# Soft-capped attention with soft mixture of experts: pairs alternating by tile, one PV pass per pair, and a five-step exponential on VectorE

## The chip, the cores and the metric

The kernel runs on one core of one Trainium2 chip. The metric is device time in microseconds, the median of several runs. The profile and the trace are of one execution; their times count from its first instruction, and the span in them (313.8 us) is about 2 us shorter than the measured time. In the text PE is the matrix engine (PEld its weight loads), ACT the engine for activations, DVE the vector engine, POOL the general-purpose one, and SP issues transfers.

## What is computed

```python
# q, k, v: (8, 12, 448, 64) float32, cap = 30
scores = q @ k.T / sqrt(64)
scores = cap * tanh(scores / cap)
attn = softmax(scores)                       # over keys
x = (attn @ v) -> (3584, 768)                # heads side by side
logits = x @ phi                             # (3584, 32): 8 experts, 4 slots each
d = softmax over tokens(logits);  slot_input = d.T @ x
h = relu(slot_input[e] @ w1[e]);  slot_out = h @ w2[e]
c = softmax over slots(logits);   out = c @ slot_out          # (3584, 768) float32
```

Almost all of the work by element is in the 8 x 12 x 448 x 448 scores, each of which needs one tanh and one exponential. As the scores are capped at 30, no maximum is subtracted.

## The kernel before

Heads are taken in pairs: 48 of them, and two pairs (four heads) make a quad `Q`, whose two pairs `h = 0, 1` lie on partitions 0-63 and 64-127 of `kT` and `qT`. A pair has NT = 7 tiles; a tile is 64 keys of each of its two heads against 448 queries. Tiles are numbered in a row, pair by pair. A chunk is CS = 3 tiles (one tanh instruction), a batch `j` is CH = 6 tiles (one exponential). There are 336 tiles, 112 chunks, NCH = 56 batches; one of the eight sequences takes PER = 7 batches.

```python
def qk_chunk(i):                               # scores of three tiles
    sc = psS.tile([P, CS, 512], F32, ...)      # two such buffers, a bank per tile
    for u in range(CS):
        pr, c = divmod(i * CS + u, NT)         # pair and tile
        Q, h = divmod(pr, 2)
        r = slice(h * HP, h * HP + HP)         # row half of the array
        for n in range(2):                     # the pair's two heads: column halves
            cs = slice(n * HP, n * HP + HP)
            pe.matmul(sc[cs, u, 0:S], qkT["k", Q][r, c, cs], qkT["q", Q][r, :, cs], ...)

def tanh_chunk(i):
    exs[j] = exps[j % 4].tile([P, CH, S], BF16)          # four buffers
    act.activation(exs[j][...], sc[...], ACT.Tanh, scale=qk_scale / cap)

def exp_chunk(j):                              # one tile fewer where DVE takes it
    exp_part(j, 1 if j in shared else 0, CH)

shared = [j for j in range(NCH - 2) if j % 7 in (1, 3) and j > 7]

def poly_exp(j, part):                         # on DVE, tile 0 of batch j, in float32
    # 7 operations: scale to a power of two in int32, mask the mantissa, mask the exponent,
    # then four multiply-adds in float32
```

"PV" is the product of the exponentials with `v`. A column of ones beside each head's `v` gives the sum for the softmax, so a head has 65 columns and a pair VW = 130. The queries are taken in NG = 4 groups of 128, of which the last begins at 320 and repeats 64 queries of the third (masked out later). A pair takes two passes of two groups, each into the one `pv` bank and each followed by its norm:

```python
GOFF = (0, 128, 256, 320)
def pv_tiles(pr, half, c0, c1, home=None):
    for c in range(c0, c1):
        for n in range(2):
            g = 2 * half + n
            pe.matmul(pvs[pr, half][:, n, 0:VW], exs[j][:, u, GOFF[g]:GOFF[g] + P],
                      vbds[Q % 2][:, h, c, :], ...)

def norm(pr, half):
    dve.reciprocal(rec, pv[:, :, :, DH:DH + 1])                          # 128 x 4
    dve.tensor_tensor(xq[Q][...], pv[:, :, :, 0:DH], rec..., op=ALU.mult)  # 128 x 256
```

The loop over the batches, in which `run(j, slot)` calls the rest of the work put into the slots (transposes of k, q and x, `logits`, `slot_sums`, loads, the parts of `poly_exp`, and `spare(n)`: n matmuls of 128 columns on ones whose result nothing uses):

```python
for j in range(NCH):
    run(j, "0")                               # e_exp, the exponential of a sequence's logits
    tanh_chunk(2 * j)
    tanh_chunk(2 * j + 1)
    exp_chunk(j - 1)                          # the first ones differ
    pv_pass(pr, 0)                            # pr: the pair whose last tile lies in batch j - 2
    run(j, "a")
    qk_chunk(2 * j + 2)
    run(j, "b")
    pv_pass(pr, 1)
    run(j, "c")
    qk_chunk(2 * j + 3)
    run(j, "d")
# then the last two pairs, the last logits and slot sums, the two layers of the experts, the output
```

Of the kernel before, what the change touches and what calls it, by code (L numbers as in the profile page):

```python
# [11 lines left out]
I32 = mybir.dt.int32  # L12
ALU = mybir.AluOpType
# [3 lines left out]
P = 128  # L17
HP = 64
# [6 lines left out]
GOFF = (0, 128, 256, 320)  # L25
VW = 2 * (DH + 1)
MASKED = -30000.0

POW2 = (0.013534163, -0.157022653, 12.3105704, 23.0539684, 37.6797712)
# [3 lines left out]
def kernel(  # L33
# [45 lines left out]
    mask = consts.tile([P, NG, NS], F32, name="mask")  # L79
    pool.memset(mask, 0.0)  # L80
    pool.memset(mask[0:HP, NG - 1, :], MASKED)
# [40 lines left out]
    for n0 in range(R2, len(blocks), 4):  # L122
        t = dram.tile([P, 2, 4, HD], BF16, name=f"w2d{n0}")
        for half in range(2):
# [3 lines left out]
    hpad = consts.tile([P, E, NFT, NS], BF16, name="hpad")  # L128

# [4 lines left out]
    px = att.enter_context(tc.tile_pool(name="px", bufs=1))  # L134

    xe, xm, xp = (px.tile([P, S], dt, name=nm)
                  for nm, dt in (("xe", I32), ("xm", F32), ("xp", F32)))
    qk = att.enter_context(tc.tile_pool(name="qk", bufs=2))
    exps, vb = [], []
    for nm, home in (("ex0", exps), ("ex1", exps), ("vb0", vb), ("ex2", exps), ("ex3", exps),  # L140
                     ("vb1", vb)):
        home.append(att.enter_context(tc.tile_pool(name=nm, bufs=1)))
# [4 lines left out]


# [124 lines left out]
    def qk_chunk(i):  # L273
        sc = psS.tile([P, CS, 512], F32, name="sc", tag="sc")
        scores[i] = sc
        for u in range(CS):
            pr, c = divmod(i * CS + u, NT)
            Q, h = divmod(pr, 2)
            r = slice(h * HP, h * HP + HP)
            for n in range(2):  # L280
                cs = slice(n * HP, n * HP + HP)
                pe.matmul(sc[cs, u, 0:S], qkT["k", Q][r, c, cs],  # L282
                          qkT["q", Q][r, :, cs], start=True, stop=True)

    def tanh_chunk(i):
        j, half = divmod(i, CH // CS)
        if half == 0:
            exs[j] = exps[j % 4].tile([P, CH, S], BF16, name="ex", tag="ex")
# [13 lines left out]
    shared = [j for j in range(NCH - 2) if j % 7 in (1, 3) and j > 7] if cap < 80 else []  # L302

    def poly_exp(j, part):
        t, bits = exs[j][:, 0, :], 2.0 ** 23
        if part == 0:
            dve.tensor_scalar(xe, t, cap * math.log2(math.e) * bits,
                              (127 + math.log2(POW2[0])) * bits, ALU.mult, ALU.add)
            dve.tensor_scalar(xm.bitcast(I32), xe, 0x007FFFFF, 0x3F800000,
                              ALU.bitwise_and, ALU.bitwise_or)  # L310
            dve.tensor_scalar(xe, xe, -0x00800000, None, ALU.bitwise_and)
        elif part == 1:
            dve.scalar_tensor_tensor(xp, xm, POW2[1], xm, ALU.add, ALU.mult)
            dve.scalar_tensor_tensor(xp, xp, POW2[2], xm, ALU.add, ALU.mult)
        else:
            dve.scalar_tensor_tensor(xp, xp, POW2[3], xm, ALU.add, ALU.mult)
            dve.scalar_tensor_tensor(t, xp, POW2[4], xe.bitcast(F32), ALU.add, ALU.mult)

    def pv_tiles(pr, half, c0, c1, home=None):

        Q, h = divmod(pr, 2)
        if c0 == 0:
            if h == 0 and half == 0:
                xq[Q] = xs.tile([P, NG, 2 * P], BF16, name="xq", tag="xq")
            pvs[pr, half] = psV.tile([P, 2, VW], F32, name="pv", tag="pv") \
                if home is None else home
        for c in range(c0, c1):
            j, u = divmod(pr * NT + c, CH)
            for n in range(2):
                g = 2 * half + n  # L330
                pe.matmul(pvs[pr, half][:, n, 0:VW],  # L331
                          exs[j][:, u, GOFF[g]:GOFF[g] + P],
                          vbds[Q % 2][:, h, c, :],
                          start=(c == 0 and n == 0), stop=(c == NT - 1),
                          skip_group_check=True)

    def norm(pr, half):
        Q, h = divmod(pr, 2)
        pv = pvs.pop((pr, half))[:, :, 0:VW].rearrange("p g (i w) -> p g i w", i=2)
        rec = xs.tile([P, 2, 2, 1], F32, name="rec", tag="rec", bufs=4)  # L340
        dve.reciprocal(rec, pv[:, :, :, DH:DH + 1])  # L341
        dve.tensor_tensor(  # L342
            xq[Q][:, 2 * half:2 * half + 2, h * P:(h + 1) * P]
            .rearrange("p g (i d) -> p g i d", i=2),
            pv[:, :, :, 0:DH],
            rec.to_broadcast([P, 2, 2, DH]), op=ALU.mult)

    def pv_pass(pr, half, home=None):
        pv_tiles(pr, half, 0, NT, home)
        norm(pr, half)  # L350


    def x_transp(pr):
        Q, h = divmod(pr, 2)
        ps = psT.tile([P, NG, P], BF16, name="xps", tag="T")
        for g in range(NG):
            pe.transpose(ps[:, g, :], xq[Q][:, g, h * P:(h + 1) * P], ident)  # L357
        t = xs.tile([P, NG, P], BF16, name="xT", tag="xT", bufs=2)
        dve.tensor_copy(t, ps)  # L359
        xTs[pr] = t  # L360

    def logits(Q, ps=None):
# [3 lines left out]
        for g in range(NG):  # L366
            for h in range(2):
                pe.matmul(ps[:, g, :], xTs[2 * Q + h][:, g, :],
                          phib[:, 2 * hq + h, :], start=(h == 0), stop=(h == 1))
# [3 lines left out]
        dve.tensor_tensor(lgs[b], ps, mask if hq == 0 else lgs[b], op=ALU.add)  # L373
# [14 lines left out]
    def e_norm(b):  # L388

        ps = psT.tile([P, 1], F32, name="zps", tag="T")  # L390
        for g in range(NG):
            pe.matmul(ps, e4s[b][:, g, :], ones[:, 0:1], start=(g == 0), stop=(g == NG - 1))
# [7 lines left out]
    def e_transp(b):  # L400

        ps = psT.tile([P, 512], BF16, name="eps", tag="T")
        for g in (3, 0, 1, 2):
            pe.transpose(ps[:, GOFF[g]:GOFF[g] + P], e4s[b][:, g, :], ident)
# [12 lines left out]
    def slot_mms(b, ps, gs, jts=None):  # L417
        for g in gs:
            for jt in range(NJ):
                pe.matmul(ps[:, jt, :],  # L420
                          xq[b * NQB + jt // 2][:, g, (jt % 2) * P:(jt % 2 + 1) * P],
                          es[b][:, g, :], start=(g == 0 and jt == 0), stop=(g == NG - 1),
                          skip_group_check=True)
# [15 lines left out]
    aux = {}  # L439
# [5 lines left out]

    def spare(n):

        busy(n, psV.tile([P, 2, VW], F32, name="junk", tag="pv")[:, 0, 0:P])

    PER = 2 * NQB * NT // CH  # L450
# [10 lines left out]
    for b in range(B):  # L461
# [3 lines left out]
        else:  # L465
            quad_in(3 * b + 1, (j - 1, "b"), (j, "a"), (j - 1, "d"), (j, "c"), (j + 1, "d"))
        quad_in(3 * b + 2, (j, "d"), (j + 1, "c"), (j + 2, "b"), (j + 2, "d"),
                (j + 4, "d"))
        quad_in(3 * b + 3, (j + 4, "a"), (j + 5, "a"), (j + 3, "d"), (j + 5, "c"),
                (j + 6, "d"))  # L470
        p = 6 * b
        at(j + 1, "d", spare, 34 if b == 0 else 10)
        at(j + 2, "d" if b == 0 else "a", spare, 4 if b == 0 else 14)
        if b:
            at(j + 2, "c", spare, 8)
        at(j + 3, "d", spare, 10 if b == 0 else 4)
        at(j + 4, "a", x_transp, p)
        at(j + 5, "a", x_transp, p + 1)
        at(j + 6, "a", x_transp, p + 2)
        at(j + 5, "d", logits, 3 * b)  # L480
        if b < B - 1:
            at(j + 7, "a", x_transp, p + 3)
            at(j + 8, "a", x_transp, p + 4)
            at(j + 7, "d", logits, 3 * b + 1)
# [334 lines left out]
```

The softmax here doesn't subtract the row's maximum and nothing guards it: scores larger than these inputs give would overflow.

## Time and profile before

| | |
|---|---|
| time, median of 3 runs | 315.84 us (315.76 to 315.91) |
| span of the profile | 313.8 us |
| PE busy | 272.0 us, 4071 matmuls |
| ACT busy | 278.9 us, 209 instructions |
| DVE busy | 191.0 us, 478 instructions |
| POOL busy | 137.5 us, 178 instructions |
| tanh | 113 instructions, 163.7 us |
| exponential of the scores | 58 instructions, 158.0 us |
| scores on PE | 672 matmuls, 78.6 us |
| PV on PE, without the first pair's second pass and the last two pairs | 1274 matmuls, 89.2 us |
| bytes moved by transfers | 67.64 MB |

The profile gives for each engine its busy time, then the span in 40 slices whose digit is the busy share in tenths, with the granted clock of PE in a row of its own; then the chain of work that ended last, by engine and by line; then the groups of instructions, each with busy time, mean duration, and the idle time of its engine just before it with what ended that. Durations of neighbouring ACT and PE instructions overlap, so the cost of one is read from start to start in the time line.

### The profile page before, as it was taken

To read this page: it belongs to the slowest core of one execution; us is meant where nothing else is said; L and a number is where in the kernel's file an instruction comes from. 1 tells how busy PE (TensorE), PEld (TensorE's weight loads), DVE (VectorE), ACT (ScalarE), POOL (GpSimd) and SP (SyncE) were. 2 spreads that over 40 slices of the span, in tenths; PEclk is the share of its full clock that TensorE was granted. 3 is DMA by queue.
4 is the path that set the end of the run, shared out by engine and by line. 5 is a ranking of instruction groups with operands and counts; after the bars stand their busy time and mean duration, and the time that the engine had idled before them with its cause. 6 is when DMAs were issued, how large, how long until landed. Compare 5 with 4: busy or idle time off the path is not lost.

```text
span 313.8 us, 9354 instructions
## 1 busy us (share of the span) xinstructions
PE 272.0 (87%) x4071; PEld 190.5 (61%) x4071; DVE 191.0 (61%) x478; ACT 278.9 (89%) x209; POOL 137.5 (44%) x178
## 2 busy tenths in 40 slices
PE   8899998989899989898989998989898898998710
PEld 6676666666676666666666666666676578643300
DVE  3624567846785578457855885578657765335830
ACT  4999999999999999999999999999999999226720
POOL 5593662655455654474457426652753020000000
PEclk9999999999999999999999999999999999999975
DMA  7999999799999999999999999999899829959996
GB/s 257 209 205 194 205 200 231 121 184 230 228 154 199 232 212 147 194 184 207 160 182 224 205 178 189 220 217 180 147 208 190 208 62 309 357 207 332 393 413 244
DMA packets 57481, 67.64 MB, mean 216 GB/s; under 512 B 3808, under 2 KB 53600, under 8 KB 57440
## 3 DMA queue, kind: packets, MB, share of 16 engines
q0 software_dynamic: 42448, 35.31, 73.5%
q1 hardware_dynamic: 14704, 31.50, 29.0%
q8 instruction: 32, 0.52, 0.6%
q10 hardware_dynamic: 288, 0.23, 0.2%
q14 instruction: 9, 0.07, 0.1%
HBM read 91.32 MB, written 18.87 MB: 351 GB/s over the span
## 4 chain that ended last, share of the span: by engine, by line
ACT 69%; PE 19%; DVE 5%; DMA 2%; issue 2%; DVEq 0%; ACTq 0%
ACT ex L291 36%; ACT ex L295 32%; PE pv L331 4%; DMA out_dram<-ob 2%; PE sc L282 2%; PE so_ps L690 2%; PE hp L662 2%; PE junk L521 2%; PE op L726 1%; PE boot L521 1%; DVE xq L342 1%; PE op L770 1%; ACT ob L779 1%; PE xps L357 1%; PE pvm L331 1%
## 5 line engine op out<-in xcount | busy, mean ns | idle before, releaser
L291 ACT ACTIVATE ex<-sc 128x1344 bf16<-128x1344 f32 (+1 forms) x113 | 163.7, 1719 | 0.8 <-PE sc L282 0.8
L295 ACT ACTIVATE ex<-ex 128x2688 bf16<-128x2688 bf16 (+4 forms) x58 | 158.0, 2753 | 0.1
L331 PEld LDWEIGHTS <-ex 128*128 128x128 bf16 x1344 | 78.0, 97 | 23.7 <-DVE xq L342 13.7
L331 PE MATMUL pv<-vbd,ex 128*128 128x130 bf16 x1274 | 89.2, 220 | 2.6 <-DVE xq L342 0.8
L282 PE MATMUL sc<-qT,kT 64*64 64x448 bf16 x672 | 78.6, 358 | 5.0 <-ACT ex L291 4.3
L260 POOL CAST vbd<-vraw 64x896 bf16<-64x896 f32 x23 | 22.4, 974 | 64.9 <-PE pv L331 49.8
L385 POOL COPY e<-E 128x512 bf16<-128x512 bf16 x9 | 6.7, 746 | 83.3 <-ACT E L379 49.2
L341 DVE RECIPROCAL rec<-pv 128x4 f32<-128x4 f32 x91 | 16.5, 182 | 42.6 <-PE pv L331 42.6
L342 DVE TENSOR_TENSOR xq<-pv,rec 128x256 bf16<-128x256 f32 x91 | 38.6, 424 | 3.1
L282 PEld LDWEIGHTS <-kT 64*64 64x64 bf16 x672 | 26.9, 105 | 22.2 <-issue 4.2
L521 PEld LDWEIGHTS <-ones 128*128 128x128 bf16 x428 | 26.0, 101 | 10.6 <-DVE xq L342 6.0
L521 PE MATMUL junk<-ones 128*128 128x128 bf16 x391 | 29.1, 220 | 3.1 <-DVE xq L342 2.6
L252 DVE COPY kT<-kps 128x896 bf16<-128x896 bf16 x23 | 14.3, 623 | 18.2 <-PE kps L250 18.0
L261 POOL CAST vbd<-vraw 64x896 bf16<-64x896 f32 x23 | 23.9, 1041 | 1.3
L109 POOL DMA_DIRECT2D w1b<-in_moe_w_dram x32 | 24.5, 766 | 0.0
L359 DVE COPY xT<-xps 128x512 bf16<-128x512 bf16 x47 | 19.5, 414 | 1.0 <-PE xps L357 1.0
L357 PE MATMUL xps<-ident,xq 128*128 128x128 bf16 x188 | 18.1, 218 | 0.8 <-DVE zacc L396 0.2
L172 POOL DMA_DIRECT2D qb<-in_q_dram x22 | 16.2, 737 | 3.9 <-DMA kraw<-in_k_dram 3.2
L252 DVE COPY qT<-qps 128x896 bf16<-128x896 bf16 x23 | 14.2, 618 | 5.5 <-PE qps L250 5.5
L250 PE MATMUL qps<-ident,qb 128*64 128x128 bf16 x308 | 12.8, 222 | 4.1 <-DVE lg L373 4.0
L172 POOL DMA_DIRECT2D kb<-in_k_dram x22 | 16.0, 727 | 0.0
L113 POOL DMA_DIRECT2D w2d<-in_moe_w_dram x20 | 15.1, 761 | 0.0
(117 smaller groups left out, 280.7 us busy)
## 6 DMA issues: line engine op xcount, KB each, us to landing
w1b<-in_moe_w_dram POOLq DMA_DIRECT2D x32, 384.0 KB, 8.5
vraw<-in_v_dram SPq DMA_DIRECT2D x23, 448.0 KB, 6.0
w2d<-in_moe_w_dram POOLq DMA_DIRECT2D x20, 384.0 KB, 9.4
w2t<-w2d SPq DMA_DIRECT2D x20, 384.0 KB, 5.2
out_dram<-ob SPq DMA_DIRECT2D x8, 768.0 KB, 8.5
qb<-in_q_dram POOLq DMA_DIRECT2D x22, 224.0 KB, 7.4
kb<-in_k_dram POOLq DMA_DIRECT2D x22, 224.0 KB, 7.8
w2b<-in_moe_w_dram POOLq DMA_DIRECT2D x12, 384.0 KB, 8.9
```

The source lines that it names most:

```text
L109: pool.dma_start(out=w1b[e][:, js, fs], in_=w1r[:, e, js, fs])
L172: (sp if nm == "v" else pool).dma_start(out=t, in_=quad_ap(nm, Q))
L252: dve.tensor_copy(t, ps)
L260: pool.tensor_copy(t[0:HP, :, :, 0:DH], raw[0:HP])
L261: pool.tensor_copy(t[HP:P, :, :, DH + 1:VW - 1], raw[HP:P])
L282: pe.matmul(sc[cs, u, 0:S], qkT["k", Q][r, c, cs], qkT["q", Q][r, :, cs], start=True, stop=True)
L291: act.activation(exs[j][:, half * CS + u0:half * CS + u1, :], sc[:, u0:u1, 0:S], ACT.Tanh, scale=qk_scale / cap)
L295: act.activation(exs[j][:, u0:u1, :], exs[j][:, u0:u1, :], ACT.Exp, scale=cap)
L331: pe.matmul(pvs[pr, half][:, n, 0:VW], exs[j][:, u, GOFF[g]:GOFF[g] + P], vbds[Q % 2][:, h, c, :], start=(c == 0 and n == 0), stop=(c == N ...
L342: dve.tensor_tensor(xq[Q][:, 2 * half:2 * half + 2, h * P:(h + 1) * P] .rearrange("p g (i d) -> p g i d", i=2), pv[:, :, :, 0:DH], rec.to_ ...
L357: pe.transpose(ps[:, g, :], xq[Q][:, g, h * P:(h + 1) * P], ident)
L521: pe.matmul(junk if home is None else home, ones, ones, start=True, stop=True)
```

## The change

It has five parts.

1. *Order of tiles.* From the second quad on, the tiles of neighbouring pairs alternate: one of a pair with `h = 0`, one of a pair with `h = 1`, and so on, so that neighbouring score matmuls lie on different row halves of the array. A pair now stretches over 13 places instead of 7, so there are five `ex` buffers instead of four. The first quad and the last pair keep their old order.
2. *PV.* A pair has one pass and one bank. Three groups of 128 queries are full; the last 64 queries of each head are a pair of small matmuls on two diagonal quarters of the array. One norm per pair. The mask for the repeated queries goes. `xq`, the transposes, logits and slot sums follow the new form (three full groups and a split one).
3. *Exponential on DVE.* Three batches in seven give a tile to DVE instead of two, and the work on it is five operations: scale to fixed point with 16 bits of fraction, shift the upper half-word into a bf16 exponent, and three multiply-adds that read the lower half-word directly.
4. *Fillers.* `fill(n)` runs n matmuls on ones into the 57 columns of the `pv` bank that a pair leaves unused, so they need no bank of their own; `spare` is used where no pair is in work. Both are there to keep PE at work between its real tasks.
5. *Slots.* Loads, casts and transposes move to the slots that the new order asks for; `e_exp` goes behind the second tanh; the buffer for the polynomial is shared with `hpad`, which is cleared at the end.

```diff
+    def turn(pr, c):
+        Q, h = divmod(pr, 2)
+        if Q == 0:
+            return pr * NT + c
+        if pr == NPAIR - 1:
+            return 2 * NTILE + c
+        at0 = 2 * NT * Q + h * NT + 2 * c
+        return at0 - 3 * (pr == NPAIR - 3 and c == NT - 1)
+    order = sorted(((pr, c) for pr in range(NPAIR) for c in range(NT)), key=lambda x: turn(*x))
+    place = {x: n for n, x in enumerate(order)}
...
-            pr, c = divmod(i * CS + u, NT)
+            pr, c = order[i * CS + u]
...
-            exs[j] = exps[j % 4].tile([P, CH, S], BF16, name="ex", tag="ex")
+            exs[j] = exps[j % NEX].tile([P, CH, S], BF16, name="ex", tag="ex")     # NEX = 5
...
+    PARTS = {1: ((0, "a", (0, 1)), (0, "d", (2, 3)), (1, "a", (4,))),
+             3: (... the same ...), 6: (... the same ...)}
+    shared = [j for j in range(NCH - 2) if j % 7 in PARTS and j > 7] if cap < 50 else []
+            lambda: dve.tensor_scalar(xe, t, cap * math.log2(math.e) * FRAC,
+                                      (127 + math.log2(lead)) * FRAC, ALU.mult, ALU.add),
+            lambda: dve.tensor_scalar(xb.bitcast(U16), whole, 7, None, ALU.logical_shift_left),
+            lambda: dve.scalar_tensor_tensor(xp, frac, p2, frac, ALU.add, ALU.mult),
+            lambda: dve.scalar_tensor_tensor(xp, xp, p1, frac, ALU.add, ALU.mult),
+            lambda: dve.scalar_tensor_tensor(t, xp, p0, xb, ALU.add, ALU.mult))
...
+    def pv_mms(pr, c0, c1, gs, dst):
+        for tail in (False, True):
+            for c in range(c0, c1):
+                for g in gs:                       # g = 3 is the tail
+                    for n in range(2 if tail else 1):
+                        r = slice(n * HP, n * HP + HP) if tail else slice(0, P)
+                        out_, v_ = (dst[r, s0, :], vbds[Q % 2][r, h, c, n * W:n * W + W]) \
+                            if tail else (dst[:, s0:s0 + 2, :], vbds[Q % 2][:, h, c, :])
+                        pe.matmul(out_, exs[j][r, u, q0:q0 + (HP if tail else P)], v_, ...)
+    def norm(pr, s0, s1, pv):                      # 128 x 7, 128 x 448
...
+    def pv_first(pr):                              # tiles 0 to 3, in place of pv_pass(pr, 0)
+    def pv_rest(pr):                               # tiles 4 to 6, the tail, the norm
+    def fill(n):
+        home = homes[max(homes)][:, NT * W:]
+        for _ in range(n):
+            pe.matmul(home, ones, ones[:, 0:512 - NT * W], start=False, stop=True)
+    FILL = ((3, "a", fill, 20), (4, "a", fill, 16), (5, "a", fill, 16), (6, "a", spare, 18),
+            (6, "c", spare, 10), (7, "a", fill, 36), (8, "a", fill, 26), (9, "a", fill, 22))
-        at(j + 1, "d", spare, 34 if b == 0 else 10)       # the old fillers of a sequence:
-        at(j + 2, "d" if b == 0 else "a", spare, 4 if b == 0 else 14)    # 10, 14, 8 and 4
...
-            at(j + 11, "0", e_exp, b)
+            at(j + 11, "e", e_exp, b)
```

## The prediction

> **What bounds the kernel now.** I read the busy table first, then the slices, then the chain, then the groups by line and the time line.
>
> ```profile
> PE 272.0 (87%) x4071; PEld 190.5 (61%) x4071; DVE 191.0 (61%) x478; ACT 278.9 (89%) x209; POOL 137.5 (44%) x178
> ACT  4999999999999999999999999999999999226720
> PEclk9999999999999999999999999999999999999975
> ACT 69%; PE 19%; DVE 5%; DMA 2%; issue 2%; DVEq 0%; ACTq 0%
> L291 ACT ACTIVATE ex<-sc 128x1344 bf16<-128x1344 f32 (+1 forms) x113 | 163.7, 1719 | 0.8 <-PE sc L282 0.8
> L295 ACT ACTIVATE ex<-ex 128x2688 bf16<-128x2688 bf16 (+4 forms) x58 | 158.0, 2753 | 0.1
> ```
>
> ACT and PE have nearly the same average, so the average decides nothing. The slices do: ACT is at 9 without a break from the second to the 34th slice, and its two groups, tanh (L291) and exponential (L295), waited 0.9 us in all, 0.8 of that for the first scores. Busy time by stretch says the same: from 16 to 260 us ACT is busy in every microsecond. PE is 87% busy but it waits for DVE (13.7 us of weight loads behind `xq`, because the PV bank is single) and for ACT (4.3 us). So until about 266 us the time is the sum of what ACT streams; after that comes a tail of some 47 us (the two expert layers, then the output's transfer), which the change hardly touches.
>
> What one instruction costs ACT must be read as start to start, because the listed durations overlap. From the time line in the middle of the run (start, duration, engine and line, count):
>
> ```profile
> 141.21 2.94 ACT L295 ACTIVATE ex<-ex 128x2688 bf16<-128x2688 bf16 x1
> ...
> 143.54 2.96 ACT L291 ACTIVATE ex<-sc 128x1344 bf16<-128x1344 f32 x2
> ...
> 145.88 2.58 ACT L295 ACTIVATE ex<-ex 128x2240 bf16<-128x2240 bf16 x1
> ...
> 147.84 2.98 ACT L291 ACTIVATE ex<-sc 128x1344 bf16<-128x1344 f32 x2
> ```
>
> Two tanh take 145.88 - 143.54 = 2.34 us; a six-tile exponential 143.54 - 141.21 = 2.33; a five-tile one (the sixth tile went to DVE) 147.84 - 145.88 = 1.96. **Moving one tile to DVE gives ACT 0.37 us.** A batch of seven iterations is 7 x 2.34 + 5 x 2.33 + 2 x 1.96 + 0.20 (the exponential of the logits, 152.51 to 152.71) = 32.15 us; the time line has 150.18 - 118.02 = 32.16.
>
> **What the skill says.** "ScalarE: Activation LUTs", section "What ACT_TABLE_LOAD costs": one element per cycle and lane whatever the function, 0.833 ns each. 448 x 0.833 = 373 ns, just the 0.37 us above, so the trace agrees and a tile less is worth that and no more. "TensorEngine Tiling (Array Packing)", section "Key Properties": different tiles of the array execute independently, and changing the tiling mode drains the engine. The trace agrees with the first and shows its size, next paragraph; no number here isolates a drain. "TensorE: Matmul & The Clock Gate", section "HAM oscillation — how this bites in real kernels": idle gaps over some 3.4 us drop the clock to half. The trace of before never shows it: the granted clock is 1.00 in every stretch up to 295 us, so the fillers there suffice. "VectorE: DVE Perf Modes", section "The perf-mode tier table": a `tensor_scalar` from SBUF gets two elements per cycle in fp32, two-tensor operations one. The trace agrees: L307 takes 383 ns and L316 615 ns for the same 448 columns.
>
> ```profile
> 145.38 0.76 PE L282 MATMUL sc<-qT,kT 64*64 64x448 bf16 x6 [0.49 <-ACT ex L291]
> ...
> 151.89 0.57 PE L282 MATMUL sc<-qT,kT 64*64 64x448 bf16 x6
> ```
>
> These are two score chunks with the same six matmuls. The 0.76 us one has its three tiles from one pair, all on one row half of the array: three steps of 0.19 us. The 0.57 us one crosses from one pair to the next, so two of its tiles lie on different row halves and run beside each other: one step fewer. That is what the new order does to almost every chunk.
>
> **The change part by part.**
>
> *Exponential.* Shared batches before: j = 8, 10, 15, 17, ... 50, 52, which is 14. The third residue, j mod 7 = 6, adds 13, 20, 27, 34, 41, 48, which is 6 (j = 6 is below the start at 8, 55 above the end). ACT: 6 x 0.37 = **2.24 us off the bounding engine**. This is all that ACT loses: tanh stays 112 chunks, `e_exp` only moves behind the second tanh.
>
> DVE: the old polynomial is seven operations, 383 + 394 + 394 + 707 + 962 + 615 + 625 ns = 4.08 us, x14 = 57 us. The new one is five: 0.38, a shift at 0.39 to 0.62 (its input steps over every second half-word; I take no packed rate for granted), three two-tensor ones at 0.62 to 0.75: 2.6 to 3.2 us, x20 = 53 to 65 us. All of it lies beside ACT.
>
> *One bank and pass per pair.* DVE: two reciprocals (182 ns) and two multiplies over 256 columns (424 ns), 1.21 us, become one of each. The multiply over 448 columns I scale by 1.04 ns a column from PSUM (the output's 128x384 takes 614 ns and its 128x768 1015): 424 + 192 x 1.04 = 0.62; a reciprocal of seven columns is 204 ns (L415). So 0.83 us, 0.38 less, x46 = 17 us off DVE. DVE as a whole goes from 191 to about 174 to 184 us. PE: 28 matmuls a pair at 58 ns ((0.97 - 0.22)/13 for a burst of 14) = 1.62 us become 21 x 58 ns = 1.22 plus 14 small ones on diagonal quarters at 26 to 50 ns (26 is the pace of the slot sums, 24 in 0.77 us): 1.6 to 1.9 us. Also the waits of PV for the previous half's norm (33 recorded, the 13.7 us above) go, as a pair's bank is read out about half an iteration before the next pair needs it.
>
> *Order of tiles.* 47 pair borders, 15 of them on a chunk border: 32 of 112 chunks cross already. Now about 101 do. 70 x 0.19 = 13 us less PE, 1.9 us a batch. Lifetimes: a pair now spans three batches of six tiles instead of two, hence the fifth `ex` buffer; the buffer is freed by the PV of the iteration before its reuse, as before, so I see no new wait of tanh on PV.
>
> *Fillers.* A batch had 10 + 14 + 8 + 4 = 36 of 128 columns at 56 ns (10 in 0.73 us) = 2.0 us. Now 136 of 57 columns at about 26 ns = 3.5 and 28 of 128 columns = 1.6: 3.1 us more PE.
>
> *PE sum per batch.* Counting only issue pace, before: scores 7.1, PV 9.7, fillers 2.0, q/k transposes 2.4, the rest 2.8: 24 us of 32.15. (Busy says 29.4 because the 0.2 to 0.36 us ends of bursts count as busy.) After: -1.9 scores, 0 to +1.7 PV, +3.1 fillers, +0.5 for split transposes, logits and slot sums: 25.7 to 27.4 us, against ACT's 32.15 - 0.37 = 31.78. PE stays under ACT, with 4 us or more a batch for latencies.
>
> *Tail.* After the last exponential PE runs a few more, smaller matmuls (slot sums 30 for 24, 0.15 us). The output transfer then moves with it. I put +0.1 us.
>
> **Sum:** 315.84 - 2.24 + 0.1 = **313.7 us**, 0.7%.
>
> **The rivals.** *(a) PE becomes the bound.* For it: PE is at 87 to 91% busy, fillers grow, and a switch between full and quartered array sits in every pair. If score chunks did not pair up and the small PV matmuls cost 58 ns each, PE would issue some 30 us a batch and, with latencies, pass 31.8: perhaps +1 us a batch, 320 us. Against it: the 0.57 us chunks, and the waits on `xq` that go. *(b) The clock falls.* The faster scores leave gaps, and at half clock PE would need some 51 us a batch; half a batch so would cost 10 us. Against it: the fillers more than replace the work saved, and no gap nears 3 us. *(c) DVE order stalls PE.* The polynomial's first step waits in DVE's queue for tanh and can hold up the copies of kT, qT or xT behind it, which free the one transpose bank. It would show as score chunks late for tanh. DVE has less work than before and each chunk has about 3 us of slack (its bank is free when tanh ends, it is needed 3.5 us later): 0 to 2 us. *(d) The gain is swallowed in the tail* because the copies of w2 into SBUF or the output transfer hold it: 315.8. Against it: these start when attention's buffers come free, which moves with ACT.
>
> **Range and chances.** The gain is arithmetic on a saturated engine and has a hard ceiling near 2.3 us, so the low side is short: 312.5. The high side has (a) and (c), some tenths to a few microseconds: 316.5. Over 2% faster needs 309.5, which nothing here gives: 0.02. Over 2% slower (above 322.2) needs (a) in full or (b): 0.07.
>
> **What would show it.** In the profile of after: ACT at 9 through the slices with waits of L291 and L295 under 1 us; 20 five-tile exponentials, 1.96 us start to start; most score chunks at 0.57 us; no PV wait on `xq`; clock 1.00 to the tail; DVE below 191 us. I would be wrong if tanh waits for `sc`, if PEclk shows anything but 9 before the tail, or if the time from the last exponential to the end differs from before by over 0.5 us.

## The result: 317.5 us, half a per cent slower

| | before | after |
|---|---|---|
| time, median | 315.81 us (315.76 to 315.91) | 317.5 us (317.02 to 322.44) |
| ratio, 95% interval | | 1.0049 [1.0033, 1.0065] |
| span of the profile | 313.8 us | 315.2 us |
| last exponential of the scores ends at | 266.45 us | 265.87 us |
| first matmul of the expert layers starts at | 270.50 us | 272.13 us |

The prediction was 313.7 us in a range up to 316.5: it missed by 3.8 us, and the time lies above the range. (The execution of 322.44 us was in a slower state of the chip, which the ratio leaves out.)

From the page of the changed kernel, the same rows as were read of before: busy time, the slices of ACT and of the granted clock, the chain that ended last by engine, and ACT's two groups.

```profile
PE 278.8 (88%) x5489; PEld 201.6 (64%) x5489; DVE 173.8 (55%) x388; ACT 277.2 (88%) x209; POOL 134.5 (43%) x176
ACT  4999999999999999999999999999999997136730
PEclk9999999999999999999999999999999999999965
PE 61%; ACT 17%; DVE 11%; POOL 3%; DMA 2%; issue 2%; DVEq 0%; ACTq 0%; POOLq 0%
L301 ACT ACTIVATE ex<-sc 128x1344 bf16<-128x1344 f32 (+1 forms) x113 | 145.8, 1414 | 1.8 <-PE pv L348 0.9
L305 ACT ACTIVATE ex<-ex 128x2688 bf16<-128x2688 bf16 (+4 forms) x58 | 137.8, 2382 | 0.1
```

ACT's row still has its nines, and its idle time is only 1.0 us more than before. On these two rows alone ACT would pass for the bound again. The chain points elsewhere: it was ACT 69% and PE 19%, it is PE 61% and ACT 17%. And of tanh's idle time one half now ends with PV, which was not so before. The chain alone proves little, though: in experiment 4 below it reads PE 47% and ACT 19%, while ACT loses next to nothing before its last exponential.

The rows of waits show a change of roles (engine and line, what it waited for, us in total, how often, the longest). Before, then after:

```profile
PE sc L282 <- ACT ex L291: 4.3, 12, 0.5
PE pv L331 <- DVE xq L342: 0.8, 2, 0.5
```

```profile
PE sc L292 <- ACT ex L301: 0.8, 2, 0.5
ACT ex L301 <- PE pv L348: 0.9, 3, 0.5
PE pv L348 <- DVE xq L356: 2.6, 13, 0.6
PE pv L348 <- POOL vbd L270: 4.8, 12, 0.7
```

PE used to wait for ACT to free a score bank, 4.3 us in all. It hardly does so any more, which makes PE itself a candidate for the bound. The longer waits of PV for the norm and for POOL's cast of `v` are not the loss: in the kernel of experiment 1, which loses nothing before its last exponential, they stand at 2.7 and 4.7 us, all but the same.

### Where the time went

Idle time hides most of it, so I took the end of every exponential of the scores and subtracted the same one of the kernel before. An end is a better witness than a duration here. ACT's records overlap, and a late start first shortens the overlap and the recorded duration (the mean tanh went from 1719 to 1414 ns in the groups above, though it does the same work) before any idle time is shown.

```
exponential of batch     13     20     27     34     35     41     42     48     49     50     51     54
after - before, us    -0.18  -0.54  -0.90  -1.27  -1.06  -1.43  -1.14  -1.50  -1.23  -1.21  -0.58  -0.58
```

Every shared batch of the third residue brings its 0.37 us, as predicted (13 to 20, 20 to 27, 27 to 34: -0.36, -0.36, -0.37); the first exponentials end 0.16 to 0.19 us later than before, so that the row begins at -0.18. But from batch 35 on something takes time back, at 35, 42, 49 and once more at 51: 0.21, 0.29, 0.27 and 0.63 us, 1.4 us in all. Of the six savings, 2.2 us, 0.58 us are left when the last exponential ends, after the start 0.19 us late and these losses.

The rest is in the tail. From the end of the last exponential to the first matmul of the expert layers it was 270.50 - 266.45 = 4.05 us and is 272.13 - 265.87 = 6.26 us: 2.21 us more. The balance of the span: -0.58 + 2.21 = +1.63, less some 0.25 us that the rest gives back, is the +1.4 us seen. The rest, from the expert layers on, computes the same in all these kernels, and in their traced executions it lies between 42.0 and 43.5 us (43.35 before, 43.09 after), so a quarter of a microsecond there says nothing.

What takes the time back shows in the time line about 136 us, in iteration 28 (start, duration, engine and line, what, count, idle time before it). The exponential is that of batch 27, a shared one:

```profile
134.66 0.86 PE L348 MATMUL pv<-vbd,ex 128*128 128x130 bf16 x12
135.36 1.12 PE L376 MATMUL pv<-ones 128*128 128x57 bf16 x36
136.01 2.54 ACT L305 ACTIVATE ex<-ex 128x2240 bf16<-128x2240 bf16 x1
136.41 0.57 PE L292 MATMUL sc<-qT,kT 64*64 64x448 bf16 x6
136.91 0.58 PE L260 MATMUL qps<-ident,qb 128*64 128x128 bf16 x14
137.42 0.96 PE L348 MATMUL pv<-vbd,ex 128*128 128x130 bf16 x19
138.36 2.55 ACT L301 ACTIVATE ex<-sc 128x1344 bf16<-128x1344 f32 x2
138.75 0.62 DVE L356 TENSOR_TENSOR xq<-pv,rec 128x448 bf16<-128x448 f32 x1
139.52 0.85 PE L348 MATMUL pv<-vbd,ex 128*128 128x130 bf16 x12 [0.70 <-POOL vbd L270]
168.62 0.57 PE L292 MATMUL sc<-qT,kT 64*64 64x448 bf16 x6
```

PE works here without a pause, and 1.1 us of it are 36 fillers (L376). Behind them come two score chunks, the q transposes and the second part of PV, which reads the oldest `ex` buffer. Tanh of the next batch writes into that buffer: it starts at 138.36, as PV's burst ends, and not 1.96 us after the exponential (137.97) but 2.35. At this place the 0.39 us still hide in the overlap; later in the run they don't. Then PE itself stands still for 0.70 us before the next pair's PV. The row names POOL's cast of `v`, but the norm's multiply ends at 138.75 + 0.62 = 139.37 and frees the one `pv` bank in the same tenth of a microsecond (the cast ended at 138.51 + 0.93 = 139.44), so both are at the limit.

The last row, out of the order of the others, is the score chunk of 136.41 one sequence, that is seven batches, later: 168.62 - 136.41 = 32.21 us. That is PE's own pace: it is 32.21 or 32.22 us for every batch from 13 to 44. ACT's exponentials at first run faster. Up to batch 34 each ends 31.93 us after the one seven batches earlier; then ACT has caught up with PE, and from batch 42 to 50 it is 32.22 us for them too. The difference, 0.29 us, is the loss of each sequence in the table. In the kernel before, both take 32.29 us.

Near the end of the run the same wait is open, on ACT's time line behind the shared batch 50:

```profile
242.04 2.09 ACT L305 ACTIVATE ex<-ex 128x2240 bf16<-128x2240 bf16 x1
244.65 2.47 ACT L301 ACTIVATE ex<-sc 128x1344 bf16<-128x1344 f32 x2 [0.52 <-PE pv L348]
```

Start to start this is 2.61 us where 1.96 were to be expected: 0.65 us, the largest of the four losses.

### The profile page after: what moved, and what is told of

It reads as the page before. It is cut to its first block, busy times and chain, and to the rows that moved or that the text cites. A ratio compares the mean times of both kernels' runs of the same rounds, so it can differ in the third digit from the quotient of the medians.

```text
span 315.2 us, 12124 instructions
## 1 busy us (share of the span) xinstructions
PE 278.8 (88%) x5489; PEld 201.6 (64%) x5489; DVE 173.8 (55%) x388; ACT 277.2 (88%) x209; POOL 134.5 (43%) x176
## 4 chain that ended last, share of the span: by engine, by line
PE 61%; ACT 17%; DVE 11%; POOL 3%; DMA 2%; issue 2%; DVEq 0%; ACTq 0%; POOLq 0%
PE pv L348 21%; ACT ex L301 9%; ACT ex L305 7%; PE pv L376 7%; PE sc L292 6%; PE junk L587 4%; DVE xq L356 4%; PE kps L260 3%; POOL vbd L270 3%; DVE xT L402 3%; PE xps L391 2%; PE qps L260 2%; DMA out_dram<-ob 2%; PE xps L396 2%; PE so_ps L752 2%; PE hp L724 2%
## 5 line engine op out<-in xcount | busy, mean ns | idle before, releaser
L301 ACT ACTIVATE ex<-sc 128x1344 bf16<-128x1344 f32 (+1 forms) x113 | 145.8, 1414 | 1.8 <-PE pv L348 0.9
L305 ACT ACTIVATE ex<-ex 128x2688 bf16<-128x2688 bf16 (+4 forms) x58 | 137.8, 2382 | 0.1
L348 PE MATMUL pv<-vbd,ex 128*128 128x130 bf16 (+1 forms) x1610 | 86.4, 210 | 9.0 <-POOL vbd L270 4.8
L348 PEld LDWEIGHTS <-ex 128*128 128x128 bf16 (+1 forms) x1680 | 72.4, 101 | 29.2 <-issue 6.6
L292 PE MATMUL sc<-qT,kT 64*64 64x448 bf16 x672 | 68.3, 359 | 1.3 <-ACT ex L301 0.8
L402 DVE COPY xT<-xps 128x448 bf16<-128x448 bf16 x47 | 18.4, 392 | 48.6 <-PE xps L396 48.6
L376 PE MATMUL pv<-ones 128*128 128x57 bf16 x1004 | 34.2, 188 | 0.0
L376 PEld LDWEIGHTS <-ones 128*128 128x128 bf16 x1004 | 31.0, 96 | 0.3
L356 DVE TENSOR_TENSOR xq<-pv,rec 128x448 bf16<-128x448 f32 x46 | 28.7, 624 | 1.6
L587 PEld LDWEIGHTS <-ones 128*128 128x128 bf16 x362 | 21.8, 102 | 6.7 <-issue 4.3
L260 PEld LDWEIGHTS <-kb 128*64 128x64 bf16 x308 | 11.1, 109 | 8.0 <-issue 7.0
```

Source lines behind the costliest of these rows:

```text
L260: pe.transpose(ps[h * HP:h * HP + HP, c, :], src[:, h, c * DH:(c + 1) * DH], ident)
L301: act.activation(exs[j][:, half * CS + u0:half * CS + u1, :], sc[:, u0:u1, 0:S], ACT.Tanh, scale=qk_scale / cap)
L305: act.activation(exs[j][:, u0:u1, :], exs[j][:, u0:u1, :], ACT.Exp, scale=cap)
L348: pe.matmul(out_, exs[j][r, u, q0:q0 + (HP if tail else P)], v_, start=(c == 0 and g == gs[0]), stop=(c == NT - 1), skip_group_check=True)
L356: dve.tensor_tensor(xq[Q][:, h, s0:s1, :], pv[:, 0:s1 - s0, 0:DH], rec.to_broadcast([P, s1 - s0, DH]), op=ALU.mult)
L376: pe.matmul(home, ones, ones[:, 0:512 - NT * W], start=False, stop=True, skip_group_check=True)
```

## The experiments

The expectations say "a batch" where they mean one sequence, some 32 us, seven of the batches numbered above.

Theory P: PE, not ACT, sets the pace of the changed kernel, and the fillers are what put it over. Rival A: ACT is still the bound, and the loss is a property of the new form (order, single PV pass, tail). Rival D: the order of work in DVE's queue holds PE up. All ratios are to the kernel before, with 95% intervals. In every kernel the computation of the output stays complete; fillers are no part of it.

### 1. Without the narrow fillers

```diff
-    FILL = ((3,"a",fill,20), (4,"a",fill,16), (5,"a",fill,16), (6,"a",spare,18),
-            (6,"c",spare,10), (7,"a",fill,36), (8,"a",fill,26), (9,"a",fill,22))
+    FILL = ((6,"a",spare,18), (6,"c",spare,10))
```

> The changed kernel without its 136 narrow fillers a batch (the 28 wide ones stay). PE theory (PE's work fills the whole batch, so tanh waits for the ex buffers that PV frees, and PE enters the tail late): PE gets 3.8 us a batch back, ACT's 1.0 us of waits go and most of the 2.2 us lost between the last exponential and the first expert layer with them: 314.5 us, between 313.8 and 315.2. Tail theory (the split form of PV, transposes and slot sums costs its 2 us in the tail whatever came before): only the 1.0 us returns, 316.4. Clock theory (the fillers are what holds PE's clock): the granted clock falls below 1.00 in the middle of the run and the time goes above 320.

Measured: 314.51 us, 0.9963 [0.9940, 0.9985], below the changed kernel's interval. The fillers cost 3.0 us by the medians, and without them the change is a small gain. (Between the two traced executions it is 2.3 us: 1.5 before the last exponential ends, 1.2 from there to the expert layers, less 0.4 in the rest.) The end of the exponentials lies at -0.21, -0.59, -0.97, -1.34, -1.71, -2.09 after batches 13, 20, ... 48 and stays at -2.10: all six savings, nothing taken back. A stretch of one sequence (stretch; its length; busy us of PE, PEld, DVE, ACT, POOL; clock; share of DMA; GB/s) of the kernel before, after, and without narrow fillers; for the last also the wait that had shrunk to 0.8, two score chunks one sequence apart, and the clock's row:

```profile
118.02:150.18 32.16, 29.26 (x454) 20.91 (x450) 21.75 (x56) 32.16 (x23) 16.95 (x21) 1.00 1.09 186
```

```profile
117.48:149.70 32.22, 29.94 (x643) 22.40 (x644) 20.10 (x45) 32.22 (x23) 17.31 (x23) 1.00 1.16 201
```

```profile
117.44:149.28 31.84, 26.79 (x505) 18.66 (x504) 20.21 (x46) 31.84 (x24) 17.12 (x22) 1.00 1.15 200
PE sc L292 <- ACT ex L301: 21.0, 31, 1.6
135.40 0.57 PE L292 MATMUL sc<-qT,kT 64*64 64x448 bf16 x6 [0.76 <-ACT ex L301]
167.32 0.57 PE L292 MATMUL sc<-qT,kT 64*64 64x448 bf16 x6 [0.76 <-ACT ex L301]
PEclk9999979999999999999999999999999999999985
```

PE has 2.5 us less to do in a sequence than before (29.26 to 26.79), of which 0.8 us are eight wide fillers fewer (2.69 to 1.91 us) and the rest is the new form; the narrow fillers give 3.15 back (29.94). Without them PE waits for ACT 21.0 us, and a sequence takes 31.84 us where the sum said 31.78. The stretch of the changed kernel, 32.22 us, is already PE's pace, though ACT's ends do not show it yet. Without narrow fillers PE repeats after 167.32 - 135.40 = 31.92 us, ACT's own pace. The clock did notice their absence once: it stood at half from 39.4 to 42.9 us (the 7 in its row), just behind a wait of PE for ACT of 1.64 us, and no exponential ended later for it.

### 2. Half of the fillers, and none at all

```diff
-    FILL = ((3,"a",fill,20), (4,"a",fill,16), (5,"a",fill,16), ..., (7,"a",fill,36), (8,"a",fill,26), (9,"a",fill,22))
+    FILL = ((3,"a",fill,10), (4,"a",fill,8), (5,"a",fill,8), ..., (7,"a",fill,18), (8,"a",fill,13), (9,"a",fill,11))
```

> The changed kernel with half of the narrow fillers. PE theory: 1.9 us a batch come back, which is more than the 0.3 us a batch that ACT waits, so it is close to the kernel without fillers, 314.5 to 315.5. Tail theory: 316.4. Clock theory: between the changed kernel and the one without fillers, or as the changed one if half is enough.

Measured: 314.42 us, 0.9961 [0.9939, 0.9984]. It can't be told from none of the narrow ones; the exponentials end 2.24 us early. So the cost of fillers isn't in proportion: the first half is free, the second half costs all of it. With this half the granted clock is 1.00 from 15 to 262 us.

> The changed kernel without narrow and without wide fillers in the batches (5.5 us of PE a batch gone). PE theory: no more than the kernel without the narrow ones, 314.5, as PE is already off the path there. Clock theory: here PE is idle often enough that the granted clock drops in the middle of the run; the time rises above 315.5 if scores then come late.

With `FILL = ()`, the `spare` ones gone too: 315.43 us, 0.9982 [0.9963, 1.0001]. The middle lies 0.9 us above the run with spares, though the two intervals overlap. The mean granted clock of its profile is 0.927, against 0.978 with the spares; the slices show where, and the two rows of waits what ACT and PE waited for:

```profile
PEclk9999799999999699879997999599966999999995
ACT ex L301 <- PE pv L348: 1.7, 5, 0.5
PE sc L292 <- ACT ex L301: 18.8, 32, 1.1
```

The fillers are not useless: without any, the clock stands at half six times ahead of the tail, 37.5 us in all, and tanh meets late PV five times. In the traced execution this takes the whole saving before the last exponential: it ends 0.28 us after that of the kernel before, not 2.09 us ahead of it. The time shows less of it because in that execution the rest of the span is 42.0 us long, 1.4 us shorter than in experiment 1; what shortened it stays open.

### 3. The changed kernel with two shared tiles in seven

```diff
-    PARTS = {1: ..., 3: ..., 6: ...}
+    PARTS = {1: ..., 3: ...}
```

> The changed kernel with two shared tiles in seven batches instead of three; ACT gets 6 x 0.37 = 2.2 us more work, DVE 6 x 2.7 us less. PE theory: ACT has slack of about that size in the changed kernel, so the time moves by less than 1 us (317.0 to 318.3). ACT theory (ACT still sets the time and something else lengthened it): +2.2 us, 319.7.

Measured: 317.95 us, 1.0065 [1.0044, 1.0085]. ACT got 6 x 0.37 = 2.2 us more to do and the time rose by some 0.45 us, within both intervals. Against rival A: where ACT is the bound its work comes back in full, as between experiments 1 and 5, which differ by the same six tiles (314.51 and 316.63 us, 2.1 us). Here it is mostly free. This kernel also tells what PE's pace of 32.2 us means: with two shared tiles ACT needs 32.3 us a sequence, PE fits under it again, and its exponentials end within 0.1 us of those of before in every batch. What all fillers cost here is 317.95 - 316.63 = 1.3 us, and it lies behind the last exponential (6.25 us to the expert layers, against 5.05 in experiment 5).

### 4. The new exponential alone, in the kernel before

The five-step polynomial and the third residue put into the kernel before; order, two PV passes and fillers as they were.

```diff
+    PARTS = {1: ((0, "a", (0, 1)), (0, "d", (2, 3)), (1, "a", (4,))), 3: (... same ...), 6: (... same ...)}
-    shared = [j for j in range(NCH - 2) if j % 7 in (1, 3) and j > 7]
+    shared = [j for j in range(NCH - 2) if j % 7 in PARTS and j > 7]
```

> The kernel before with the exponential on 16-bit halves for three tiles a batch and nothing else of the change. PE theory: the kernel before leaves PE 2.7 us a batch of waits, so all of the 6 x 0.37 = 2.2 us is seen, 313.6. DVE theory (five-step polynomials in DVE's queue hold up the copies PE waits for): 315 or more.

Measured: 314.23 us, 0.9951 [0.9932, 0.9971]. One of the five parts, alone, does better than all five. The exponentials end 2.01 us early. From there to the expert layers it is 269.13 - 264.46 = 4.67 us, 0.6 more than before: ACT came 2 us earlier to the tail, and PE, with 87% busy, did not quite follow (PV's last burst starts 0.59 us ahead of the end of the last exponential, before 1.23 us ahead).

### 5. The new form alone

Experiment 1 with two shared tiles instead of three: order, PV form and slots are new, ACT's work is that of before.

> The changed kernel without the narrow fillers and with two shared tiles in seven batches, so the new order and the new PV by themselves beside the old number of tiles on DVE. If these two cost the batches nothing and the tail about 1 us (as the kernel without narrow fillers shows from the last exponential to the experts' first layer): 316.7, that is 2.2 us over that kernel. If they cost the batches too: above 317.3. If they are free, as the prediction had it: 315.9.

Measured: 316.63 us, 1.0034 [1.0016, 1.0051], as expected from a cost in the tail alone. Its exponentials end within 0.2 us of those of before in every batch, so through the batches the new form costs nothing, and it gives PE time: it waits for ACT 21.4 us. It costs 5.05 us instead of 4.05 from the last exponential to the expert layers. So +1.0 us of the tail is the form itself. The traces divide it: the last norm ends 1.88 us after the last exponential before and 2.22 us here, and from there to the expert layers it takes 2.17 and 2.83 us. So one third lies in PV and two thirds in what follows it, the split transposes, logits and slot sums. With all fillers the whole stretch is 6.26 us, without the narrow ones 5.06: the other 1.2 us is PE's lateness under the fillers, as PV's last burst starts 1.34 us after the last exponential with them and 0.15 us without.

The parts together, by medians: exponential alone -1.6, form alone +0.8, both -1.3, both with fillers +1.7.

### 6. The tail's small matmuls gathered

In the last pair full and small PV matmuls alternate in short groups. On top of half the fillers:

```diff
-    for half, gs in enumerate(halves):
-        pv_mms(last, NT - 1, NT, gs, pv2[half])
-        norm(...)
+    pv_ends(0, NT - 1)                      # the twelve small ones, in one group
+    pv_mms(last, NT - 1, NT, (0, 1), pv2[0]); norm(...)
+    pv_mms(last, NT - 1, NT, (2,), pv2[1]); pv_ends(NT - 1, NT); norm(...)
```

> The changed kernel with half of the narrow fillers, and in the last pair the small PV matmuls gathered: twelve in one group before the last exponential ends and two after it, instead of three groups between full ones, so four changes of the array's form fewer. If a change of form costs some 0.1 to 0.2 us as the tail's bursts suggest (15 matmuls in 1.05 us, of which 9 full ones at 58 ns are 0.52): 0.3 to 0.6 us less than with half of the fillers alone, 313.8 to 314.1. If the cost lies in the number of matmuls: no difference, 314.4.

Measured: 314.09 us, 0.9941 [0.9909, 0.9974]; 0.3 us below the same kernel ungathered, which the intervals don't separate. The trace has it at 4.83 us instead of 5.05 for the stretch. The size is that of the lower end of what was expected. All of the 0.2 us lies ahead of the last norm's end (1.99 us after the last exponential, where it was 2.22); the 0.7 us behind it is not touched by this edit.

### 7. Five tiles in seven, in the new form and in the old

If only fillers stood in the way, ACT could be relieved further: residues 1, 3, 4, 5, 6 with half the fillers, and the same five in the kernel before.

> The changed kernel with half of the narrow fillers, and a tile to DVE in five batches of seven (residues 1, 3, 4, 5, 6) instead of three. ACT loses 13 or 14 more tiles, some 5.0 us. PE theory (the new order and the single PV pass free PE, the fillers spent it): with PE relieved ACT sets the time again and all of it is seen, 309.5 (309.0 to 310.5). If DVE's longer queue holds up the copies PE waits for: 311.5 or more.

> The kernel before with the same five tiles a batch to DVE and nothing else of the change. ACT theory (the old PV and the old order are no limit): 309.2, as 5 us more leave ACT. PE theory: the old form keeps PE at 29.4 us of work and some waits in a batch that ACT would now do in 31.1, so a part of the 5 us is lost in waits of tanh and in a late entry into the tail: 311 to 313.

Measured: 322.34 us, 1.0212 [1.0128, 1.0295], and 334.25 us, 1.0564 [1.0502, 1.0626]. The first confirms what was said for a longer DVE queue (311.5 or more), the second is more than 20 us above both its forecasts: theory P alone does not carry this far. Waits of the first, then of the second:

```profile
ACT ex L301 <- PE pv L350: 6.7, 9, 1.0
PE qps L260 <- DVE xT L404: 6.0, 5, 1.5
```

```profile
PEld L340 <- DVE xq L351: 27.4, 43, 1.4
ACT ex L293 <- PE pv L340: 17.2, 13, 2.0
```

In both, PE waits for DVE and ACT for PE. DVE is busy 66 and 70% only, which points not to its load but to what stands ahead of what in its queue. In the old form every pair needs its norm twice to free the `pv` bank, and it is these waits (27.4 us) that lead; the single pass per pair has fewer of them (5.1 us in 13 of its weight loads). So at five tiles the new form is 12 us the better of the two; that its fewer norms are the reason is read from the waits, and no run took the single pass alone.

### 8. Four tiles: the same amount of work at two places

To test rival D by itself: the kernel of experiment 6 with a fourth residue, which is 4 in one run and 2 in the other. ACT and DVE get the same work (27 five-tile exponentials, 423 DVE instructions in both), only the place in DVE's queue differs.

```diff
     PARTS = {1: ..., 3: ..., 6: ...,
+             4: ((0, "a", (0, 1)), (0, "d", (2, 3)), (1, "a", (4,)))}     # run "four"
+             2: ((0, "a", (0, 1)), (0, "d", (2, 3)), (1, "a", (4,)))}     # run "fourb"
```

> The changed kernel with half of the narrow fillers, the gathered tail, and a fourth shared tile in seven batches, at the residue 4, so that the two batches around the transposes of the next quads (5 and 0) stay free of it. If the loss with five tiles came from DVE's queue in just those batches: ACT loses 7 x 0.37 = 2.6 us more and the time is 311.5 (311.0 to 312.3). If any neighbouring pair of shared batches holds PE up: above 314.1.

Measured: 316.25 us, 1.0010 [0.9984, 1.0036], nearly 5 us above the first forecast and on the side of the second (neighbouring shared batches). The time line at 97 us shows a cause:

```profile
96.82 0.95 POOL L271 CAST vbd<-vraw 64x896 bf16<-64x896 f32 x1
97.05 1.20 DVE L329 SCALAR_TENSOR_TENSOR work<-work 128x448 f32<-128x448 uint16 x1
97.85 0.22 PE L397 MATMUL xps<-ident,xq 64*64 64x64 bf16 x2
98.28 0.63 DVE L330 SCALAR_TENSOR_TENSOR work<-work 128x448 f32<-128x448 f32 x1
98.83 0.38 DVE L403 COPY xT<-xps 128x448 bf16<-128x448 bf16 x1
99.26 0.58 PE L260 MATMUL qps<-ident,qb 128*64 128x128 bf16 x14 [0.82 <-DVE xT L403]
100.65 2.47 ACT L301 ACTIVATE ex<-sc 128x1344 bf16<-128x1344 f32 x2 [0.87 <-PE pv L349]
```

The last x transposes end at 98.07. Their copy, which frees the one transpose bank, starts only at 98.83, behind two steps of the polynomial; the q transposes wait for the bank 0.82 us, PV stands behind them in PE's queue, and tanh waits 0.87 us for PV. Over the run this wait of the q transposes is 6.3 us in 6.

The queue alone does not explain it. The step at 97.05 takes 1.20 us, where the same step elsewhere takes 0.62, and POOL's cast of `v` runs beside it from 96.82 to 97.77. Of the 81 multiply-add steps of this run 11 take 1.04 to 1.40 us, each beside a cast or a copy on POOL; the other 70 take about 0.62 us. Ahead of five of the six waits (0.76 to 1.52 us) stand one or two such stretched steps, and what they are too long by (0.6 to 1.4 us) is nearly the whole wait. So residue 4 is a bad place for two reasons together, and no run parts them.

The clock has a share in the traced execution, which at 318.52 us is 2.3 us above the median: right behind the first and longest wait (1.52 us, to 64.04) it stands at half from 65.2 to 72.0 us, and the exponentials of batches 12 to 14 lose 3.2 us, where the two other waits of 1.5 us (to 131.39 and 195.03) cost 0.5 to 0.6. It isn't the whole: the five executions with a mean granted clock of 0.985 to 0.987, that of the next run, take 314.87 to 318.11 us, median 315.92.

> The same as the kernel with a fourth shared tile at the residue 4, but at the residue 2 in its place. With residue 4, the third and fourth step of the polynomial stood in DVE's queue ahead of a copy of xT, and the transpose of the next q in the same iteration waited for that copy's bank. After residue 2 comes an iteration with an x transpose but no transpose of q or k. If that position is the cause: 2.6 us less than with the gathered tail alone, 311.5 (311.0 to 312.3). If any fourth tile overloads DVE or any two neighbouring shared batches do: 314 or more.

Measured: 311.91 us, 0.9882 [0.9866, 0.9899], as forecast from the position, and faster than both kernels; here three neighbouring batches (residues 1, 2, 3) are shared, so neighbours as such do no harm. At residue 2 there are no q or k transposes behind the steps. Eight steps are stretched here too (1.04 to 1.07 us), but the wait of `qps` for `xT` is gone from its list, and its exponentials end 5.04 us before those of the kernel before. From its page and its waits:

```profile
PE 265.3 (86%) x4987; PEld 188.0 (61%) x4987; DVE 192.4 (62%) x423; ACT 274.1 (89%) x209; POOL 133.5 (43%) x176
ACT 58%; PE 25%; DVE 9%; issue 2%; DMA 2%; DVEq 0%; SPq 0%; ACTq 0%
PE sc L292 <- ACT ex L301: 4.4, 8, 1.1
```

ACT leads the chain again, and PE waits for it 4.4 us, as much as in the kernel before. Whether the kernel before could have taken residue 2 as well was not tried.

## Why the prediction was wrong

**The exponential: right.** Twenty five-tile exponentials; a third tile gives 0.36 to 0.37 us; six of them 2.24 us in the ends of experiment 1, from +0.15 at the start to -2.09 (2.24 predicted). The new polynomial takes 401 + 433 + 615 + 625 + 618 ns = 2.69 us (2.6 to 3.2 predicted), the wider norm 624 ns and the reciprocal 205 (620 and 204), and DVE is busy 173.8 us (174 to 184 in the prediction; its own terms, -17.5 and -4 to +8 on 191, give 170 to 182).

**The form on PE: right in direction.** Score matmuls went from 78.6 to 68.3 us of busy time, 10 us where I had 13 (103 of 112 chunks take 0.56 to 0.63 us instead of 31, but many of them 0.63), and without narrow fillers PE's busy time falls by 2.5 us a sequence.

**The PE sum: the step that failed.** "Counting only issue pace, before: ... 24 us of 32.15. (Busy says 29.4 because the 0.2 to 0.36 us ends of bursts count as busy.)" I threw out the ends of bursts as if they were an artefact, got 25.7 to 27.4 us after, and concluded "PE stays under ACT, with 4 us or more a batch for latencies". Measured, there was no such slack. PE repeats itself after 32.21 us with all fillers, and ACT needs 31.92 (by the ends of its instructions; the 31.78 is from start to start): not 4 us of room, but 0.3 too little. What the change adds was foreseen well, +1.7 to +3.4 us: by tiles, in the two stretches of a sequence, scores are 1.3 us less, PV 0.5 less, fillers 3.8 more, and the transposes of x, logits and slot sums 1.1 more, +3.1 in sum (these times overlap, PE's busy time grows by 0.7). The base they were set on was wrong. Before, PE was busy 29.26 of 32.16 us, so 2.9 us were free and not 8; setting my own additions on the profile's 29.4 would have given 31.1 to 32.8 us against 31.78: no room. That it is the ends of bursts that can't be used is an inference, as no run changes them alone. What the runs show is that PE at 26.79 us busy a sequence waits for ACT, and 3.15 us more, to 29.94, make it the slower of the two.

The fillers' pace was right (36 make a burst of 1.12 us, of which the last one's own duration is 0.19, so 26.6 ns each, where I had 26). My rival (a) is what happened. It named PE's 87 to 91% and the growing fillers, but looked for the overrun in chunks that fail to pair up and in slow small matmuls, neither of which occurred (eight of the small ones take 0.29 us).

**The buffers: a second failed step, in consequence.** "The buffer is freed by the PV of the iteration before its reuse, as before, so I see no new wait of tanh on PV." The distance is the same, but with a PE that is later the buffer is freed later: four losses of 1.4 us in all. "Also the waits of PV for the previous half's norm go" failed too, in part: of the 13.7 us of weight loads behind the norm 4.2 are left, and PV's own wait for it, the row shown above, grew from 0.8 to 2.6 us (with 4.8 more under POOL's name). As said above, these cost nothing where PE has time.

**The tail: mis-sized.** "I put +0.1 us" was 2.2 us: 1.0 for the split form, of which I had counted only the slot sums' extra matmuls, and 1.2 for PE's lateness. I looked for the path to the end behind ACT alone, but between the last exponential and the experts PE is the path. On the form's part, the Trainium skill's "TensorEngine Tiling (Array Packing)", section "Key Properties", says that a change of tiling mode drains the engine; the prediction had left that without a size. Gathering the small matmuls saved 0.2 us in the trace, and no run isolates a drain, so the agreement is one of direction only.

**The clock: right.** 1.00 up to 295 us in the changed kernel. That its fillers "more than replace the work saved" was true as well, and was the trouble. The Trainium skill's page cited for it, "TensorE: Matmul & The Clock Gate", section "HAM oscillation — how this bites in real kernels", speaks of idle gaps over some 3.4 us. Here shorter pauses were enough, and the measurement decides: in the run without any filler (0.927 against 0.978) the clock fell to half six times, although PE's longest pause between 15 and 262 us was 1.1 us, the row shown above. That "no gap nears 3 us", as rival (b) had it, was no safeguard; the fillers were.

**The rival on DVE's order** named what is held up, the copy of xT that frees the transpose bank, but not what holds it: not the first step's wait for tanh, but later steps that POOL's casts stretch. At three tiles it did not occur (no step of the changed kernel is stretched); at four with residue 4 it is part of 4.3 us against residue 2.

What stays open: which of the split transposes, logits and slot sums costs the 0.7 us behind the last norm; whether the queue or POOL's casts weigh more at residue 4; and why the rest of the span varies by up to 1.4 us between executions.

## What to carry to other kernels

When a kernel's bound is relieved, set the second engine's busy time, with the ends of its bursts, against the new period, and not against the old; 94% with a chain of buffers behind it was already too much here. The pace of an engine can be read directly: take one of its instructions and the same one a period later. Fillers belong only in time that their engine has to spare; here half of them held the clock and cost nothing. And judge a move to an idle engine by what stands behind it in that engine's queue and by what runs beside it on others: the same tile brought its full gain at one place and cost 4.3 us more at another.

## What was not expected of the hardware

ACT's recorded durations swell while it never waits and shrink as soon as it does: in the kernel before, the six-tile exponential is listed at 2.44 us at the start of the run, 2.94 at 141 us and 3.35 at 246 us, for the same 2.33 us start to start; in the changed one, behind the late waits, it is at 2.44 us again (237.36 us). A wait of 0.39 us hid so at 138.36 us, with no idle time shown. Periods read from starts come out short while the records swell: 32.17 us a sequence before, against 32.29 by the ends, which is also PE's.

A multiply-add of VectorE over 448 float32 columns takes 0.62 us alone and up to 1.40 us beside a cast on POOL; so the kernel before paid 962 ns on average for one of its steps (L314) and 615 for an equal one (L316). In the kernel with residue 4 the norms, which read the PSUM bank, keep their 0.62 us beside the same casts.

And a matmul of 57 columns on ones is not free: 36 of them took 1.12 us.
